# Batching two more chunks of y@w_ch, and sending the seventh chunk's spreads after the last modes

## The chip, the cores and the metric

One core of one Trainium2 chip. A profile is one execution with the hardware profiler on. Its span is shorter than the device time of the same execution, by 1.7 us for the kernel before (453.8 and 455.52), so spans are compared with spans and times with times.

Engines: PE is the matmul engine, ACT the scalar, DVE the vector engine, POOL GpSimd, SP the engine that issues most transfers. SPq, POOLq and DVEq are those engines' sequencers. PSUM is the memory that the matmuls of this program write to; tiles whose names end in _ps lie in it.

## The reference

Causal attention, then a spectral mixing on its output x (8 batches, 576 positions, 512 features, 64 Fourier modes), then a residual with a ReLU:

```python
X = np.fft.rfft(x, axis=1)
# per mode: complex product of X[:, :64] with w_r + i w_i
y = np.fft.irfft(Y, n=S, axis=1)
u = x + y
return u + np.maximum(u @ w_ch, 0.0)
```

The kernel never forms y in time before the product: it computes y@w_ch in the frequency domain and transforms both back.

## The kernel before

The 64 modes are treated in eight chunks, whose weights stream in all the time (the page has the DMA busy 90% or more in the first 36 of its 40 slices). The last feature group yields, for each chunk, a tile `y_sb` of 128 rows (mode, real or imaginary, batch). Two things are needed of it: y itself, and v = y@w_ch, both "spread" so that the modes lie in the partitions of one tile `yv` (16 partitions per chunk, batches along the free axis). Then the inverse transforms are matmuls with `yv` as weights.

There are two ways into `yv`. A chunk can compute its own v and send both by transfers of 128 KB:

```python
if c >= NCK - 2:
    spread(c, 0, yb)           # at the end of modes(): y of the last two chunks
...
def spread(c, which, rows):
    nc.sync.dma_start(out=yv[16 * c : 16 * c + 16, :, which, :], in_=rows)
...
def y_times_wch(c, yt):        # v of one chunk: 4 matmuls, one DVE copy, one transfer
    ...
    nc.vector.tensor_copy(out=vb, in_=vp)
    spread(c, 1, vb)
    return vb
```

Or `gather` takes several chunks' transposed y and makes the rows of `yv` by matmul, batch by batch, each in its own band of partitions, so that no transfer is needed; a round of it is 16 (or 8) matmuls into one PSUM tile and four (or two) copies out of it, on ACT and DVE in turn. Chunks one to four go that way altogether, chunks five and six with y alone:

```python
for c in range(NCK - 2):
    yb = modes(NG - 1, c)
    ...
    yt = y_transposed(yb, c)
    ...
    if c >= NY:
        y_times_wch(c, yt)
        if c == NCK - 3:
            gather(NY, NCK - 2, (), (0,))     # y of chunks five and six, two rounds
    elif c == NY - 1:
        gather(0, NY, (1, 3), (1, 0))         # v and y of chunks one to four
...
c = NCK - 2                                   # the seventh chunk
x_times_wch(0, False)
yb6 = modes(NG - 1, c)
x_transposed(1)
yt = y_transposed(yb6)
x_times_wch(1, False)
vb6 = y_times_wch(c, yt)
...
yb = modes(NG - 1, NCK - 1, {2: first_u, 3: first_z})   # the eighth chunk
```

The first output tiles take chunks seven and eight straight from their tiles (96 rows of `yv` are enough); the first "full" inverse transform reads all 128 rows, and so waits for every spread.

The softmax here doesn't subtract the row's maximum and nothing guards it: scores larger than these inputs give would overflow.

## Time and profile before

| | before |
|---|---|
| time, us (median of 3; range) | 456.47 (455.56 to 456.91) |
| time of the profiled execution | 455.52 |
| span of the profile | 453.8 |
| last matmuls of chunk four's modes start (weights set the pace up to here) | 372.85 |
| modes of chunk five start | 390.79 |
| modes of the eighth chunk start | 411.04 |
| first full inverse transform starts | 421.99 |

The last four rows cut the tail of the kernel into stages. Each is the start of one line of PE's timeline. The chain and the timeline of the batch are shown in the prediction. The transfers from 417 to 425 us: the eighth chunk's two spreads, with the time from issue to landing in the last column.

```profile
yv<-y_sb SPq DMA_DIRECT2D x1, 128.0 KB, 2.9
yv<-v_sb SPq DMA_DIRECT2D x1, 128.0 KB, 2.9
```

### The profile page before, as it was taken

Reading aid. Unit: us, or ns where it says so; the run is one execution under the profiler, and the core shown is the slowest. Engines: PE = TensorE matmul, PEld = TensorE weight load, DVE = VectorE, ACT = ScalarE, POOL = GpSimd, SP = SyncE. Lnnn points to the kernel's source line nnn. Section 1 sums busy time; section 2 is a strip of 40 time slices with the busy share of each in tenths; the row PEclk is TensorE's granted clock in tenths of the full one; section 3 lists DMA queues with packets and bytes.
Section 4 is the critical chain, followed back from the end, with each engine's and each line's share of the span. In section 5 each row is a group of like instructions: output and inputs, shape, how many; then the busy total and the mean of one; then the engine's idle time right before and its main releaser. Section 6 shows DMA issues by size and latency. Waiting matters only on the chain.

```text
span 453.8 us, 10370 instructions
## 1 busy us (share of the span) xinstructions
PE 340.4 (75%) x4233; PEld 218.6 (48%) x4265; DVE 241.0 (53%) x535; ACT 221.9 (49%) x390; POOL 183.0 (40%) x269
## 2 busy tenths in 40 slices
PE   1779887976563979836677857688889678879995
PEld 1456665654342656624445535456554335534332
DVE  7775665753242656723436434446655443562796
ACT  1585877464242656724435444455551323431774
POOL 6655554554344565434364444444433231200000
PEclk9996999998576889968878899889996986999999
DMA  9999999999999999999999999999999999995688
GB/s 176 200 203 203 202 201 204 202 204 204 205 204 202 201 203 202 205 205 204 202 196 203 204 204 203 204 203 202 206 207 208 207 206 206 207 214 109 232 298 317
DMA packets 108511, 93.75 MB, mean 207 GB/s; under 512 B 28384, under 2 KB 103648, under 8 KB 108464
## 3 DMA queue, kind: packets, MB, share of 16 engines
q0 software_dynamic: 98960, 81.81, 113.8%
q1 hardware_dynamic: 9504, 11.29, 7.8%
q8 instruction: 33, 0.54, 0.4%
q14 instruction: 14, 0.11, 0.1%
HBM read 164.56 MB, written 9.44 MB: 383 GB/s over the span
## 4 chain that ended last, share of the span: by engine, by line
DMA 51%; PE 31%; DVE 8%; issue 4%; POOL 2%; ACT 2%; SPq 0%; DVEq 0%; POOLq 0%; ACTq 0%
DMA w_sb<-in_moe_w_i_dram 21%; DMA q<-in_q_dram 15%; DMA w_sb<-in_moe_w_r_dram 11%; PE sc_ps L365 4%; PE av_ps L394 4%; PE z_ps L602 3%; PE yp L441 3%; PE sc_ps L359 3%; PE tr_ps L324 3%; DMA k<-in_k_dram 2%; PE z_ps L693 2%; PE g_ps L652 2%; PE ft_ps L418 2%; PE u_ps L712 2%; PE u_ps L693 1%
## 5 line engine op out<-in xcount | busy, mean ns | idle before, releaser
L373 ACT ACTIVATE p_sb<-sc_ps,cumt_sb 128x576 f16<-128x576 f32 (+1 forms) x256 | 141.7, 635 | 45.6 <-PE sc_ps L365 45.0
L217 POOL DMA_DIRECT2D w_sb<-in_moe_w_i_dram x60 | 45.1, 751 | 85.0 <-PE yp L441 37.6
L217 POOL DMA_DIRECT2D w_sb<-in_moe_w_r_dram x60 | 45.3, 757 | 63.5 <-DMA w_sb<-in_moe_w_r_dram 28.2
L217 POOL DMA_DIRECT2D v<-in_v_dram x72 | 50.8, 708 | 32.0 <-DMA w_sb<-in_moe_w_r_dram 7.4
L324 PE MATMUL tr_ps<-ident,q 64*64 64x64 bf16 x576 | 17.5, 210 | 54.3 <-DMA q<-in_q_dram 54.3
L359 PE MATMUL sc_ps<-negm,ident 128*128 128x256 bf16 x256 | 55.5, 303 | 0.2
L327 DVE COPY qtA<-tr_ps 64x576 bf16<-64x576 bf16 x32 | 23.8, 743 | 49.6 <-PE tr_ps L324 49.5
L441 PE MATMUL yp<-w_sb,xs 128*32 128x512 bf16 x480 | 36.5, 406 | 14.1 <-DMA w_sb<-in_moe_w_i_dram 11.1
L344 ACT ACTIVATE p<-sc_ps,cumt 128x64 f16<-128x64 f32 x32 | 10.0, 313 | 74.3 <-PE sc_ps L340 74.3
L394 PE MATMUL av_ps<-v,p_sb 128*128 128x65 f16 x1024 | 44.5, 198 | 0.0
L394 PEld LDWEIGHTS <-p_sb 128*128 128x128 f16 x1024 | 39.5, 100 | 4.9 <-issue 0.8
L327 DVE COPY ktA<-tr_ps 64x576 bf16<-64x576 bf16 x32 | 24.0, 749 | 33.6 <-PE tr_ps L324 33.6
L324 PEld LDWEIGHTS <-q 64*64 64x64 bf16 x576 | 13.7, 123 | 57.0 <-DMA q<-in_q_dram 56.3
L365 PE MATMUL sc_ps<-qtB,ktB 128*128 128x64 bf16 (+2 forms) x160 | 34.9, 324 | 3.5 <-issue 2.4
L365 PE MATMUL sc_ps<-qtA,ktA 65*128 65x512 bf16 (+2 forms) x192 | 36.5, 299 | 0.7 <-DMA qtA<-ncum_sb 0.7
L399 DVE TENSOR_REDUCE den<-av_ps 128x5 f32<-128x10 f32 x64 | 10.8, 169 | 49.1 <-PE av_ps L394 48.9
L441 PEld LDWEIGHTS <-xs 128*32 128x32 bf16 x512 | 22.6, 170 | 23.8 <-issue 19.8
L404 DVE TENSOR_TENSOR x_all<-av_ps,rcp 128x320 f16<-128x320 f32 x64 | 31.5, 491 | 2.2
L327 ACT COPY ktB<-tr_ps 64x576 bf16<-64x576 bf16 x32 | 20.3, 634 | 20.3 <-DVE ktA L327 19.4
L365 PEld LDWEIGHTS <-ktB 128*128 128x128 bf16 x192 | 22.4, 117 | 14.8 <-issue 6.3
L324 PE MATMUL tr_ps<-ident,k 64*64 64x64 bf16 x576 | 17.3, 209 | 15.3 <-DVE qtB L327 10.7
L602 PE MATMUL z_ps<-wch_sb,xs 128*128 128x512 f16 x96 | 26.1, 421 | 0.2 <-DVE xs L596 0.2
(117 smaller groups left out, 534.8 us busy)
## 6 DMA issues: line engine op xcount, KB each, us to landing
w_sb<-in_moe_w_r_dram POOLq DMA_DIRECT2D x60, 512.0 KB, 11.9
w_sb<-in_moe_w_i_dram POOLq DMA_DIRECT2D x60, 512.0 KB, 11.9
q<-in_q_dram POOLq DMA_DIRECT2D x32, 144.0 KB, 9.9
k<-in_k_dram POOLq DMA_DIRECT2D x32, 144.0 KB, 10.0
v<-in_v_dram POOLq DMA_DIRECT2D x72, 64.0 KB, 9.7
out_dram<-r_sb SPq DMA_DIRECT2D x16, 256.0 KB, 2.2
out_dram<-r_w SPq DMA_DIRECT2D x16, 256.0 KB, 2.6
x_all<-in_moe_w_i_dram POOLq DMA_DIRECT2D x3, 512.0 KB, 9.9
```

Of the source, the lines that this page charges most:

```text
L217: nc.gpsimd.dma_start(out=dst, in_=src)
L324: nc.tensor.transpose(ps[rows, r, :], src[rows, r, :], ident16[rows, rows])
L327: copy(out=dst[n % NQ][rows, :].rearrange("d (p r) -> d p r", r=R), in_=ps[rows].rearrange("d r p -> d p r"),)
L359: nc.tensor.matmul(ps[:, bass.ds(w * S, W)], ident16, negm[:, bass.ts(r, W)], start=True, stop=False, skip_group_check=True,)
L365: nc.tensor.matmul(ps[:, c0 : c0 + i1 - i0], keys[:, w, r, :], qt[:, i0:i1], start=False, stop=True, skip_group_check=True,)
L373: nc.scalar.activation(out=pt[:, poff[x] : poff[x] + S - w * W], in_=ps[:, w * S : (w + 1) * S - w * W], func=ACTF.Exp, bias=cumt_sb[:, x, ...
L394: nc.tensor.matmul(ps[:, I, r : r + NCH], lhsT, rhs, start=(i == 0), stop=(i == len(todo) - 1), skip_group_check=True,)
L399: nc.vector.tensor_reduce(out=den, in_=ps[:, :, 0 : VW : NCH], axis=mybir.AxisListType.X, op=ALU.add)
L404: nc.vector.tensor_tensor(out=x_all[:, g, b, :, D * h : D * h + D], in0=ps[:, :, 1 : NCH], in1=rcp.unsqueeze(2).to_broadcast([P, NT, D]), ...
L441: nc.tensor.matmul(ps[32 * cg : 32 * cg + 32, :], cols[:, c0 : c0 + 32, c * MC + 2 * cg + par], wt[(g, c, ri, par)][:, cg, :], start=(x == ...
L602: nc.tensor.matmul(z[:, x, :], xts[i][:, x, dt, :], wch_sb[:, dt, :], start=(dt == 0), stop=(last and dt == DT - 1), skip_group_check=True,)
L693: nc.tensor.matmul(dst[x][r, :], G_sb[rows, bass.ds(T * P, r.stop - r.start)], yv[rows, bb, which, :], start=start, stop=True, skip_group_ ...
```

## The change

Intent: v of chunks five and six made in the batch too, so that two copies and two transfers among the weights go away; the batch cut into single rounds, put where PE has gaps; and the seventh chunk's two transfers kept out of the stream of weights, since nothing needs them before the first full transform. Core of the diff (cuts marked):

```diff
-            if c >= NCK - 2:
+            if c == NCK - 1:
                 spread(c, 0, yb)
...
         nc.vector.tensor_copy(out=vb, in_=vp)
-        spread(c, 1, vb)
         return vb
-    def gather(c0, c1, turns, kinds):
+    def gather(c0, c1, r, which):            # one round of one kind
...
-                    if g % 2:
-                        nc.vector.tensor_copy(out=dst, in_=src)
...
+            if g == ng - 1:
+                nc.vector.tensor_copy(out=dst, in_=src)
+            else:
+                nc.scalar.copy(out=dst, in_=src)
...
-        if c >= NY:
-            y_times_wch(c, yt)
-            if c == NCK - 3:
-                gather(NY, NCK - 2, (), (0,))
...
+        elif c == NCK - 3:
+            gather(NY, NCK - 2, 0, 1)
+            gather(NY, NCK - 2, 0, 0)
...
     c = NCK - 2
     x_times_wch(0, False)
+    gather(NY, NCK - 2, 1, 1)
     yb6 = modes(NG - 1, c)
     x_transposed(1)
+    gather(NY, NCK - 2, 1, 0)
...
     yb = modes(NG - 1, NCK - 1, {2: first_u, 3: first_z})
+    spread(NCK - 2, 0, yb6)
+    spread(NCK - 2, 1, vb6)
```

More of the change, by code (lines that the diff above doesn't have):

```diff
@@ L645, in gather @@
         ng = P // n
-        for b0 in range(0, B, ng):
-            for which in kinds:
-                ps = auxpool.tile([P, DM], FP32, name="g_ps", tag="aux")
-                for dt in range(DT):
-                    for g in range(ng):
-                        op = yt_first[:, dt, : c1 - c0].rearrange("p c (x b) -> p (c x) b", b=B)
-                        nc.tensor.matmul(
-                            ps[n * g : n * g + n, :] if which else ps[n * g : n * g + n, bass.ts(dt, P)],
-                            op[:, :, b0 + g],
-                            wch_sb[:, dt, :] if which else ident16h,
-                            start=(dt == 0 or not which), stop=(dt == DT - 1 or not which),
-                            tile_position=(0, n * g), skip_group_check=True,
-                        )
-                for g in range(ng):
-                    dst, src = yv[rows, b0 + g, which, :], ps[n * g : n * g + n, :]
-                    if g % 2:
-                        nc.vector.tensor_copy(out=dst, in_=src)
-                    else:
-                        nc.scalar.copy(out=dst, in_=src)
-            if b0 // ng in turns:
-                work()
+        ps = auxpool.tile([P, DM], FP32, name="g_ps", tag="aux")
+        op = yt_first[:, :, : c1 - c0].rearrange("p d c (x b) -> p d (c x) b", b=B)
+        for dt in range(DT):
+            for g in range(ng):
+                nc.tensor.matmul(
+                    ps[n * g : n * g + n, :] if which else ps[n * g : n * g + n, bass.ts(dt, P)],
+                    op[:, dt, :, r * ng + g],
+                    wch_sb[:, dt, :] if which else ident16h,
+                    start=(dt == 0 or not which), stop=(dt == DT - 1 or not which),
+                    tile_position=(0, n * g), skip_group_check=True,
+                )
+        for g in range(ng):
+            dst, src = yv[rows, r * ng + g, which, :], ps[n * g : n * g + n, :]
+            if g == ng - 1:
+                nc.vector.tensor_copy(out=dst, in_=src)
+            else:
+                nc.scalar.copy(out=dst, in_=src)
     ahead = []
@@ L763 @@
             work()
-        if c >= NY:
-            y_times_wch(c, yt)
-            if c == NCK - 3:
-                gather(NY, NCK - 2, (), (0,))
-        elif c == NY - 1:
-            gather(0, NY, (1, 3), (1, 0))
+        if c == NY - 1:
+            for r in range(4):
+                gather(0, NY, r, 1)
+                gather(0, NY, r, 0)
+                if r % 2:
+                    work()
+        elif c == NCK - 3:
+            gather(NY, NCK - 2, 0, 1)
+            gather(NY, NCK - 2, 0, 0)
     assert not order_z and not ahead
```

## The prediction

> **What bounds the kernel now.** I read the chain of waits first, for which resource sets the end in the stretch the change touches; then the timeline of that stretch, engine by engine; then the issues and landings of its transfers.
>
> The page's summary of the chain, then the chain itself from chunk four on (start us, us, what):
>
> ```profile
> DMA 51%; PE 31%; DVE 8%; issue 4%; POOL 2%; ACT 2%; SPq 0%; DVEq 0%; POOLq 0%; ACTq 0%
> ```
>
> ```profile
> 353.00 19.81 DMA w_sb<-in_moe_w_i_dram
> ...
> 396.37 0.92 DVE y_acc L495
> 397.61 0.50 issue
> 398.11 0.69 DVE y_sb L455
> 399.24 1.73 PE z_ps L602 x8
> 400.97 0.86 PE v_ps L633 x4
> 402.29 0.58 ACT yv L664
> 402.89 0.70 DVE yv L662
> 403.61 0.58 ACT yv L664
> 404.22 0.69 DVE yv L662
> 404.94 0.70 DVE yv L662
> 405.66 0.58 ACT yv L664
> 406.27 0.71 DVE yv L662
> 407.00 0.69 DVE y_sb L455
> ```
>
> Weights set the pace up to 372.8 us; nothing of that half is changed. From there TensorE (PE) [...]waits on short hand-offs. Between chunks six and seven the chain is the eight evacuation copies of the batched y (`gather`), strictly one after the other: ScalarE (ACT), VectorE (DVE), ACT, DVE. `y_sb` of chunk seven stands behind the last of them. So the end is set here by PSUM evacuation, not by matmul work or by a transfer.
>
> The timeline of the same place shows what each costs:
>
> ```profile
> 395.13 1.03 PE L633 MATMUL v_ps<-wch_sb,yt_first 128*128 128x512 f16 x4
> 396.08 1.12 PE L441 MATMUL yp<-w_sb,xs 128*32 128x512 bf16 x16
> 397.51 0.68 DVE L637 CAST v_sb<-v_ps 128x512 f16<-128x512 f32 x1
> 401.01 1.01 ACT L492 COPY z<-z_ps 128x1024 f32<-128x1024 f32 x1 [1.09 <-PE z_ps L602]
> 401.76 0.47 PE L652 MATMUL g_ps<-ident16h,yt_first 128*32 128x128 f16 x16
> 403.61 1.17 ACT L664 CAST yv<-g_ps 32x512 f16<-32x512 f32 x2 [0.75 <-DVE yv L662]
> 404.97 1.12 PE L441 MATMUL yp<-w_sb,xs 128*32 128x512 bf16 x16
> 411.04 0.69 PE L441 MATMUL yp<-w_sb,xs 128*32 128x512 bf16 x8
> ```
>
> A 32-partition copy of 512 columns takes 0.58 us on ACT and 0.69 on DVE, no less than one of 128 partitions: cutting a tile into four rows quadruples the evacuation.
>
> The last weight tile. The list of DMA issues, asked for 396 to 397.5 us, gives issue to landing:
>
> ```profile
> w_sb<-in_moe_w_i_dram POOLq DMA_DIRECT2D x1, 512.0 KB, 18.3
> ```
>
> It is issued at 396.87, so it lands near 415.17; its matmuls start at 415.30. PE gets there at the same moment (the 0.42 us before them is put down to "issue", as at other changes of tile width, and not to the DMA). The tile before it, 18.0 us from 393.96, lands near 411.96 and is used at 413.06. So two resources are nearly level: an earlier PE alone would gain about 0.1 us, and an earlier last weight alone gains nothing.
>
> [...]16 matmuls of 32 columns take 1.12 us, the four copies of a round about 2.6. [...]this program guards the whole tile: ACT and DVE never overlap on one tile in the trace. [...]a 128 KB spread takes 6.0 and 6.5 us to land beside the weights, and 2.9 us when they are done.
>
> **The change part by part.** The first batch (chunks one to four) keeps its order on every engine; its two copies per round still go to ACT and DVE. Nothing up to 395.13 moves.
>
> *Chunks five and six lose y@w_ch of their own.* Removed: 2 x 4 matmuls of 512 columns (0.86 us of PE each), 2 DVE copies (0.60 us each back to back) and 2 spreads of 128 KB. Chunk six's modes start 0.86 us earlier, 395.22. But their `y_sb` stands on DVE behind the subtraction that waits for ACT (395.33 + 1.01) and frees DVE only at 397.51. The only thing saved is the `v_sb` copy: `y_sb` starts at 397.51 instead of 398.11, minus 0.60.
>
> *The batch does it instead, in four rounds.* Added: 2 x 16 matmuls of 32 x 512, like those of the modes (1.12 us), so PE is about 0.4 us worse off in all. Copies go from 8 to 16 and are no longer split evenly: three of each four are ACT's (12 x 0.58 = 7.0 us), the fourth is DVE's and waits for ACT's third. The new order on the engines, worked through with the durations above:
>
> PE: transposes of chunk six 398.25, z 398.48, round A (product) 400.30 to 401.42, round B (y) to about 401.85, z of pair 0 to 403.5. ACT: the kept z 400.41 to 401.42, then A 401.48 to 403.23, B 403.23 to 404.98. DVE's fourth: A 403.26 to 403.95, B 405.01 to 405.70.
>
> There are two auxiliary PSUM buffers, so round C (product) may start when A is emptied, 404.00 to 405.12, and the modes of chunk seven when B is, at 405.75 (before: 404.97, so 0.78 late). ACT C 405.18 to 406.93, DVE C 406.96 to 407.65. The built order puts `y_sb` of chunk seven behind DVE C: 407.57 instead of 407.00. Round D (y) on PE 407.70 to 408.17; ACT D 408.23 to 409.98, and only then ACT's transposed copy of chunk seven, done at 410.56. PE meanwhile does pair 1's z from 408.9 to 410.63, so of ACT's delay nothing is left: v of chunk seven starts at 410.63 (before: 410.08), and the last chunk's modes at 411.58 (before: 411.04). Sum: -0.60 gained at `y_sb` of chunk six, +1.14 lost in the copies, net +0.54 us.
>
> *The spreads.* Four of 128 KB leave the stream of weights, two for good and two moved behind the last modes. At the 207 GB/s of that stretch each is 0.63 us, so the last weight should land some 2 to 2.5 us earlier, near 413. It is used at 415.84 by the new times: the relief is real, but hidden. The delayed pair is put between the eighth chunk's y and its v on SyncE's queue, 0.55 us of issue each. The eighth chunk's v was issued at 418.72 and landed 2.9 us later, 421.62, with its reader's weights loaded at 421.77: 0.15 us to spare. Two more transfers stand ahead of it, about 0.5 to 0.7 us of engine time each; as they are issued 0.55 us apart, most is through before it. I allow 0.1 us of new wait.
>
> Sum: +0.54 + 0.1 = about +0.6 us in the profiled execution. What follows 421.7 is unchanged, with PE busy 9.25 of 9.30 us up to 431, so a delay is carried to the end. I take 0.2 off, because in executions other than the profiled one the last weight may be the later of the two and the relief then counts: 456.47 + 0.4 = 456.9 us.
>
> **The rivals.**
>
> *The last weight is what really binds.* It lands within about 0.1 us of its use, and executions of before differ by 1.35 us (455.56 to 456.91). If it is usually late by 1 us, the change turns that wait into slack and PE's +0.54 is what remains: up to 0.5 us faster, 456.0. Against it: no wait for the last weight is charged in this trace.
>
> *Copies overlap better than I worked out.* If ACT keeps ahead and PE's fillers cover the rounds, only -0.60 remains: 455.9. Against it: the two-buffer rule and the order on DVE are built in, and each round must hold a buffer for some 2.4 us.
>
> *ACT becomes the bound.* 12 copies plus the kept z are 8 us in a stretch of about 10; if hand-offs are longer than the 0.03 to 0.06 us seen, each round adds to it and chunk seven's transposed copy delays v: +1.5 us, 458.0.
>
> *The delayed spreads hold up the first full inverse transform.* If the eighth chunk's v queues behind both, it lands 1.0 to 1.3 us late: 457.5 to 458.
>
> **Range and chances.** The parts are all below 1.5 us, against 9.1 us for 2%. The range, 455.4 to 458.3, is the worst rivals on either side plus the spread of single executions. Faster by over 2%: 0.01; within 2%: 0.98; slower by over 2%: 0.01.
>
> **What would show it.** In the timeline: `y_sb` of chunk six near 397.5 and not 398.1 (step one); four rounds of copies of about 2.4 us each, modes of chunk seven near 405.75 and those of chunk eight near 411.6, with the wait before chunk seven put down to a DVE copy of yv; ACT busy nearly throughout from 400.4 to 410.6. In the list of issues: the last weight landing 2 us or more ahead of its use; the eighth chunk's v landing about 3 us after issue. I am wrong if the last chunk's modes start before 410.5 or after 412.5, if the end moves by over 2 us, or if the first half moves at all: the grant of TensorE's clock (0.71 from 372.9 to 390.8) could do that without any of this.

General statements that no trace of this case shows are cut from it. No term of its sum is among them: +0.54 for `y_sb` and the copies, +0.1 for the delayed spreads, about +0.6 in the profiled execution; less 0.2, +0.4 in time. That a copy of 32 partitions takes no less than one of 128 is read off the same profile: ACT's 32x512 copies took 574 ns on average and its 128x512 ones of the transposed y 588; DVE's took 690 and, for v, 687.

## More of the kernel before

The metric is device time in microseconds (us), the median of several executions.

PE's timeline at the first full inverse transform (`128*128`; start us, us). It names no wait: the matmuls before it end just as it starts.

```profile
421.12 1.03 PE L827 MATMUL z_ps<-r_sb,ident16h 128*128 128x512 f16 x4
421.99 0.59 PE L693 MATMUL z_ps<-yv,G_sb 128*128 128x512 f16 x2
```

What SP waits for at the end of the program, after its last store is issued (from 444 us on; us in total, times, longest us):

```profile
SPq L879 <- DMA out_dram<-r_sb: 1.6, 3, 0.6
```

And two rows of the page's table of DMA queues (packets, MB, share of 16 engines):

```profile
q8 instruction: 33, 0.54, 0.4%
q14 instruction: 14, 0.11, 0.1%
```

The page calls their kind `instruction` and counts them with the same 16 DMA engines as the data: 33 packets of 16 KB (q8) and 14 of 8 KB (q14). They are taken here for the engines' own instructions on their way in, and called fetches: q8's for PE's, q14's for other engines', SP's among them. The rows do not say so; runs that change PE's or SP's count test it (e10, x1, x3).

## The result, and the profile after

The changed kernel takes 459.25 us (458.17 to 460.6, six runs), beside 456.54 (455.56 to 457.51, six runs) for the kernel before. The ratio is 1.006, with an interval of 1.0037 to 1.0082. (Ratios here are the mean time of one kernel's fast runs over that of the other's of the same rounds, so not quite the ratio of the medians quoted.) That is within 2%, as predicted, but +2.7 us where +0.4 was predicted, and above the range (455.4 to 458.3). Results are correct.

The page's summary of the chain, to be held against "DMA 51%; PE 31%; DVE 8%" of before:

```profile
DMA 57%; PE 29%; DVE 5%; ACT 3%; issue 3%; POOL 2%; DVEq 0%; POOLq 0%; ACTq 0%
```

DVE's share shrank and DMA's grew. The timeline of the changed kernel, line by line against the prediction: `y_sb` of chunk six, the row of ACT copies, the modes of chunks seven and eight, and the first full inverse transform.

```profile
397.63 0.68 DVE L455 TENSOR_TENSOR y_sb<-yp,y_acc 128x512 f16<-128x512 f32 x1
401.56 5.42 ACT L661 CAST yv<-g_ps 32x512 f16<-32x512 f32 x9
405.86 1.12 PE L441 MATMUL yp<-w_sb,xs 128*32 128x512 bf16 x16 [0.68 <-DVE yv L659]
411.78 0.69 PE L441 MATMUL yp<-w_sb,xs 128*32 128x512 bf16 x8
424.17 0.60 PE L688 MATMUL z_ps<-yv,G_sb 128*128 128x512 f16 x2 [1.28 <-DMA yv<-v_sb]
```

The first four are within 0.2 us of the predicted 397.51, 401.48, 405.75 and 411.58. The fifth carries a wait of 1.28 us that was not there before, and the chain of waits goes through it:

```profile
419.45 4.67 DMA yv<-v_sb
424.12 0.05 issue
424.17 0.60 PE z_ps L688 x2
```

The eighth chunk's v needs 4.67 us to land instead of 2.9. So far that is rival four. But the end is later as well. The stages:

| stage, us | before | after | difference |
|---|---|---|---|
| chunk five's modes to the eighth's | 20.25 | 20.88 | +0.63 |
| eighth's modes to first full transform | 10.95 | 12.39 | +1.44 |
| first full transform to the end | 31.81 | 32.43 | +0.62 |
| sum | | | +2.69 |

The sum is the difference of the medians (2.7; the two spans differ by 2.8). The half before (372.85 and 372.71 for chunk four's last matmuls) did not move. In the last stage PE does the same work in the same time (busy 26.06 us before, 26.07 after); what differs is SP's wait for the last stores, the same view as before:

```profile
SPq L882 <- DMA out_dram<-r_sb: 2.3, 3, 1.1
```

The longest wait is 1.1 us, was 0.6. The stores land late (those from r_sb of 256 KB 2.7 us after issue in the median, 2.2 before). Asked for half a microsecond at a time, the list of transfers has one instruction packet in each of the two places: the first line is of 421 to 421.5 us, in the middle of the spreads; the second of 451 to 451.5, on the first of the last four stores (issued at 450.89).

```profile
q8 instruction: 1, 0.02, 22.4%
...
q14 instruction: 1, 0.01, 4.4%
```

By their records in the trace the first packet took 1.79 us (22.4% of 16 x 0.5) and the second 0.35 (4.4%). In the kernel before the same fetches fall at 423.5 to 424 (1.73 us), when its last spread had landed (421.6), and at 446.5 to 447 (0.40 us), ahead of the last four stores (448.70). The other 32 packets of q8 took 0.89 to 1.05 us in both traces. The change has 46 more PE instructions and four fewer SP instructions (8594 to 8640, 236 to 232 in the built programs). The theory is that this shifts where in the work each next fetch falls. Not shown is how a fetch would hold up a transfer, and the trace does not name the engine of a packet, so this link is the author's guess; that the landing is late when such a packet falls on it is what the runs test.

### The profile page after: what moved, and what is told of

Its sections match the earlier page's. It is cut to its first block, busy times and chain, and to the rows that moved or that the text cites. A ratio compares the mean times of both kernels' runs of the same rounds, so it can differ in the third digit from the quotient of the medians.

```text
span 456.6 us, 10452 instructions
## 1 busy us (share of the span) xinstructions
PE 344.5 (75%) x4289; PEld 218.5 (48%) x4289; DVE 239.2 (52%) x533; ACT 227.0 (50%) x398; POOL 183.2 (40%) x269
## 4 chain that ended last, share of the span: by engine, by line
DMA 57%; PE 29%; DVE 5%; ACT 3%; issue 3%; POOL 2%; DVEq 0%; POOLq 0%; ACTq 0%
DMA w_sb<-in_moe_w_i_dram 29%; DMA q<-in_q_dram 13%; DMA w_sb<-in_moe_w_r_dram 5%; PE yp L441 5%; PE sc_ps L365 4%; PE av_ps L394 3%; PE sc_ps L359 3%; DMA x_all<-in_moe_w_r_dram 2%; DMA k<-in_k_dram 2%; PE tr_ps L324 2%; PE z_ps L688 2%; DMA y_acc<-in_moe_w_i_dram 2%; PE ft_ps L418 2%; DMA y_acc<-in_moe_w_r_dram 2%; PE z_ps L514 2%
## 5 line engine op out<-in xcount | busy, mean ns | idle before, releaser
L365 PE MATMUL sc_ps<-qtB,ktB 128*128 128x512 bf16 (+2 forms) x192 | 44.8, 351 | 0.0
L324 PE MATMUL tr_ps<-ident,k 64*64 64x64 bf16 x576 | 17.5, 210 | 14.1 <-DVE qtB L327 10.1
```

The costliest lines, as they stand in the source:

```text
L324: nc.tensor.transpose(ps[rows, r, :], src[rows, r, :], ident16[rows, rows])
L365: nc.tensor.matmul(ps[:, c0 : c0 + i1 - i0], keys[:, w, r, :], qt[:, i0:i1], start=False, stop=True, skip_group_check=True,)
```

## The experiments

Theories. **Copies** (C in the texts): the four-quadrant copies cost 0.63. **Row** (Q): four spreads in a row slow one another. **Fetch** (F): the displaced instruction fetches cost some 0.6 each, on the eighth chunk's v and on the last stores. Two more letters stand in the texts: W and R, that the relief of the last weights is worth something. The rival to all is what the total alone would suggest: the new batch costs 2.7 us, being longer than worked out. The stages of all runs are in one table at the end of this section.

### e1_early_spreads and e2_late_spreads: the two halves of the change apart

e1 is the changed kernel with the seventh chunk's spreads at their old places:

```diff
-            if c == NCK - 1:
+            if c >= NCK - 2:
                 spread(c, 0, yb)
...
+        spread(c, 1, vb)
         return vb
...
-    spread(NCK - 2, 0, yb6)
-    spread(NCK - 2, 1, vb6)
```

e2 is the kernel before with only these two spreads late:

```diff
-            if c >= NCK - 2:
+            if c == NCK - 1:
                 spread(c, 0, yb)
...
-        spread(c, 1, vb)
+        if c < NCK - 2:
+            spread(c, 1, vb)
...
+    spread(NCK - 2, 0, yb6)
+    spread(NCK - 2, 1, vb6)
```

> The changed kernel with the seventh chunk's two spreads put back where they were (each issued as soon as its rows are ready); the batch in four rounds stays. Theory Q (queue): most of the 2.7 us come from the four spreads standing in one row, which let the eighth chunk's v land 4.67 us after issue instead of 2.9; with the row gone it lands in about 2.9 us, the wait of 1.28 us before the first full inverse transform is gone, the last chunk's modes stay near 411.8, and the time is 0.5 to 1.0 us over before (456.5), so near 457.2. Theory C (copies): the sixteen copies and ScalarE's load cost the time, now or through what follows; then it stays 2 us or more over before. Theory W (weights): the delay of the spreads was worth something by letting the last weight land earlier; then the last weight lands after 415 again and a wait for it appears.

> The kernel before with only the seventh chunk's two spreads delayed behind the last modes; y@w_ch of chunks five and six as before. Theory Q: the eighth chunk's v lands 4 to 5 us after issue, PE waits 1.2 to 2 us for it, and the time is 1.5 to 2.2 us over before. Theory C: no more than 0.5 us over before, since no copy is added. Theory W: faster than before by some 0.1 us or more.

e1: 457.99 us, ratio 1.0027 (1.001 to 1.0043). e2: 456.93, ratio 1.0008 (0.9991 to 1.0024). The late spreads alone are not 2 us, and without them half the loss stays. In e2's profile the full transform waits 0.69 us; its stage is 0.85 us longer than before, and the end is not (31.80). In e1, with a single spread of v as before, it still waits. The lines of e2 and of e1:

```profile
423.20 0.61 PE L694 MATMUL z_ps<-yv,G_sb 128*128 128x512 f16 x2 [0.69 <-DMA yv<-v_sb]
```

```profile
422.79 0.60 PE L689 MATMUL z_ps<-yv,G_sb 128*128 128x512 f16 x2 [0.54 <-DMA yv<-v_sb]
```

e1's v took 3.9 us to land instead of 2.9, with no other spread near. What was near: v was issued at 418.81, and from 419.5 to 420 us the only packet on the engines is an instruction fetch, which starts just ahead of the spread's own packets and takes 1.5 us (18.8% of 16 x 0.5).

```profile
DMA packets 1, 0.02 MB, mean 33 GB/s; under 512 B 0, under 2 KB 0, under 8 KB 0
...
q8 instruction: 1, 0.02, 18.8%
```

So the row of four costs 0.85 (e2), and something else that goes with the new batch costs 0.7 at the same place and 0.6 at the end (e1: 32.41, longest wait for a store 1.1).

### e4_doubled and e5_wide: what is slow in a row of four

Both are the kernel before with its early spreads kept, plus two transfers of 128 KB after the last modes: e4 sends the narrow ones (16 partitions) a second time, e5 sends the same tiles whole, into 128 partitions of a spare tile.

```diff
+    spread(NCK - 2, 0, yb6)                                    # e4
+    spread(NCK - 2, 1, vb6)
```

```diff
+    for i, src in enumerate((yb6, vb6)):                       # e5
+        nc.sync.dma_start(out=y_acc[:, 4 + i, : DM // 2].bitcast(FP16), in_=src)
```

> The kernel before with the same two spreads issued a second time behind the last modes (same rows, same values; the early ones stay). The relief of the weights is away, the row of four at the end is there. Theory Q: as late as the run with only the delay, 1.5 to 2.2 us over before. If the relief of the weights matters, it is slower than that run by what the relief is worth. Theory C: at most 0.3 us over before.

> The kernel before with two extra transfers of 128 KB at the same place, from the same tiles, but into 128 partitions of a spare tile instead of 16. It tells two forms of theory Q apart. Q1: what holds the eighth chunk's v is the number of bytes and packets ahead of it in the queue; then it lands as late as with the doubled spreads (4 us or more after issue) and costs the same 1.5 us or so. Q2: what holds it is that many rows go into few partitions, which a single spread hides and a row of four doesn't (packets went from about 60 to 160 ns in the changed kernel's trace); then wide transfers let it land in 2.9 to 3.5 us and cost under 0.7 us.

e4: 456.87, 1.0006 (0.9992 to 1.0021); e5: 456.29, 0.9998 (0.9974 to 1.0021). The times are too close; the profiles are not. e4's full transform waits 0.66 us, e5's not at all (10.96, as before). (e4's stage is 12.65: it also holds waits of 0.41 and 0.35 us for the last two weights, which come back below.) The lists of transfers of e2 and of e5, 417 to 425.4 us in 40 slices of 0.21 us, show the rate:

```profile
GB/s 0 0 0 0 0 49 205 283 112 190 283 122 210 185 112 112 107 98 127 102 102 68 205 195 176 322 361 419 410 400 380 419 400 410 419 302 234 49 0 0
```

```profile
GB/s 0 0 0 0 0 0 0 0 0 0 0 24 161 288 147 258 297 59 302 293 44 0 137 254 220 15 0 0 68 419 380 429 371 419 380 234 380 410 420 439
```

In e2 the first half of the row goes mostly at 185 to 283 GB/s, and then eight slices in a row at about 105. The trace of the changed kernel, which has the same row, shows it packet by packet: from the middle of the third narrow spread on, the 1 KB packets take 145 to 167 ns (means of 64 records), against 49 to 64 in the first. In e5, with the wide ones in between, each of the four peaks at 250 to 300 and is through, with pauses between them. So what slows is several narrow spreads without a pause, not the bytes and not the issues. Why the narrow ones slow is not shown.

### e6_pe_shift, e8_both_shift, e9_before_shifted: instruction counts moved, clumsily

e6 is the changed kernel with 23 small transposes of the attention part, far ahead, done twice (46 PE instructions). e8 adds six SP instructions. e9 is the kernel before with the same 23 transposes, and four SP loads moved to ACT's queue.

```diff
                 nc.tensor.transpose(ps[rows, r, :], src[rows, r, :], ident16[rows, rows])
+                if n == 6 and 2 * r + h < (12, 11)[which]:                  # e6, e8, e9
+                    nc.tensor.transpose(ps[rows, r, :], src[rows, r, :], ident16[rows, rows])
...
-    nc.sync.dma_start(out=ident16h, in_=d_ident16h)
+    for _ in range(5):                                                      # e8
+        nc.sync.dma_start(out=ident16h, in_=d_ident16h)
...
+    nc.scalar.dma_start(out=ident16h, in_=d_ident16h)                       # e9 (and Ff_sb, G_sb, ident32)
```

> The changed kernel with 46 harmless instructions more on TensorE, early, where it waits for transfers (23 transposes of the seventh head pair done twice). Theory F (fetch): the change, by its 46 more TensorE instructions, moved one 16 KB transfer of TensorE's own instructions (queue 8 of the profile) onto the spread of the eighth chunk's v[...]; 46 more move it ahead of the spreads. Then the eighth chunk's v lands about 4.1 us after issue (as with the delayed spreads alone) instead of 4.7, PE's wait shrinks from 1.28 to about 0.7 us, and the time is 0.4 to 0.8 us below the changed kernel's 459.25, near 458.6. Theory Q alone: no change, within 0.3 us. Extra work costs: slower than the changed kernel.

> As the run before it, and SyncE given six instructions more, early (a small constant loaded four times again), so that the last 8 KB transfer of instructions (queue 14), which in the changed kernel and in the one with early spreads fell among the last stores, comes before them again. Theory F: from the first full inverse transform to the end of the span 31.8 us again (as before) instead of 32.4; the time another 0.4 to 0.7 us lower, near 458.0, that is 1.3 to 1.7 us over before: 0.6 of copies and 0.8 of the row of four spreads are left. Theory Q alone: no change against the changed kernel.

> The kernel before, with nothing of the change, but with the instruction counts of the changed kernel: 46 more on TensorE (early, repeated transposes) and 4 fewer on SyncE (four constants loaded from ScalarE's queue). Theory F: the eighth chunk's v lands 3.7 us or more after issue, a wait of about 0.5 us for it appears, the end after the first full inverse transform takes 32.4 us instead of 31.8, and the time is 0.8 to 1.3 us over before, near 457.5. Without theory F: within 0.3 us of before.

e6: 459.34, 1.0064 (1.0044 to 1.0084). e8: 460.15, 1.0079 (1.0056 to 1.0102). e9: 456.45, 1.0000 (0.9983 to 1.0017). All three totals missed what the fetch theory expected. In e6 the shift put the fetch just ahead of the row instead of on it, and the wait stayed 1.11. In e8 chunk four's last matmuls start at 376.91, not 372.7, presumably because of the five loads at the very start, so its total cannot be read; and a fetch of PE fell among the stores at 448.69 us, 12 us before the end. In e9 the profile shows all that the fetch theory expected (v landing 3.9 us after issue, a wait of 0.53 for it, 32.32 us to the end), and a wait of 1.02 us for a weight besides:

```profile
412.97 0.45 PE L443 MATMUL yp<-w_sb,xs 128*32 128x512 bf16 x4 [1.02 <-DMA w_sb<-in_moe_w_i_dram]
```

Yet e9's time is that of the kernel before; why is not known. A shift has to be aimed: the same count as before but for a whole block, the instructions of one packet, and by a means that costs nothing at the front. The block was taken as 256 PE instructions. That is the author's estimate: 33 packets of q8 for 8594 instructions (before) and for 8640 (after) are one for every 260 and 262.

### e10_before_pe46 and e11_after_aligned: the shift aimed

e10 is the kernel before with just the 46 more PE instructions, one per call. e11 is the changed kernel with 210 more (46 + 210 = 256, one block by that estimate, so the fetches should fall where they did in the kernel before) and four more SP instructions, by cutting two small transfers of two heads in two. (The cut transfers bring two PE instructions more, so the built program has 258 over the kernel before.)

```diff
                 nc.tensor.transpose(ps[rows, r, :], src[rows, r, :], ident16[rows, rows])
+                if 0 < n and 2 * r + h < 1 and 1 * (2 * n - 2 + which) + 2 * r + h < 23:    # e10
+                if 0 < n and 2 * r + h < 2 and 2 * (2 * n - 2 + which) + 2 * r + h < 105:   # e11
+                    nc.tensor.transpose(ps[rows, r, :], src[rows, r, :], ident16[rows, rows])
...
-        nc.sync.dma_start(out=qtA[n % NQ][D : D + 1, :], in_=ncum_sb[p0 : p0 + 1, :])
+        for cols in (slice(0, S // 2), slice(S // 2, S)) if n in (5, 6) else (slice(0, S),):   # e11
+            nc.sync.dma_start(out=qtA[n % NQ][D : D + 1, cols], in_=ncum_sb[p0 : p0 + 1, cols])
```

> The kernel before with only 46 TensorE instructions more (23 transposes done twice, one at a time, spread over the first half), so that the 16 KB transfer of TensorE's instructions falls where it falls in the changed kernel. Theory F: the eighth chunk's v lands 3.7 to 4.0 us after issue, and from the start of chunk eight's modes to the first full inverse transform it takes 11.5 to 11.8 us instead of 10.95; from there to the end 31.8 as before, because SyncE's count is untouched; the time 0.5 to 0.9 us over before. Without F: 10.95 and the time within 0.3 us of before.

> The changed kernel with the instruction counts brought back to where before has them modulo the size of a fetch: 210 more on TensorE (105 transposes done twice, two at a time over the first half), 4 more on SyncE (four tiny row loads cut in two). The last shifts failed because one transfer fell just ahead of the row of spreads, and another among the stores. Theory F: 11.8 us from chunk eight's modes to the first full inverse transform (12.39 in the changed kernel; the row of four alone gave 11.80) and 31.8 from there to the end (32.43); the time 1.0 to 1.5 us below the changed kernel, 457.7 to 458.2. Without F: as the changed kernel, 459.3.

e10: 457.12, ratio 1.0012 (0.9995 to 1.0029). Nothing near the end of this kernel differs from the kernel before, and yet its full transform waits; the list of transfers has v landing after 3.9 us, and a fetch between 422 and 422.5.

```profile
424.62 0.60 PE L695 MATMUL z_ps<-yv,G_sb 128*128 128x512 f16 x2 [0.49 <-DMA yv<-v_sb]
```

The stage is 12.31, a miss (11.5 to 11.8 was expected): PE also waits for the last two weights, as it does not in the profile of the kernel before. After these, from the transposes of the eighth chunk's y to the full transform, it takes 6.33 us for 5.68 before, so 0.65 of the 1.36 by which the stage grew is the fetch's. The end is as before (31.78).

```profile
414.77 0.46 PE L443 MATMUL yp<-w_sb,xs 128*32 128x512 bf16 x4 [0.36 <-DMA w_sb<-in_moe_w_i_dram]
417.31 0.45 PE L443 MATMUL yp<-w_sb,xs 128*32 128x512 bf16 x4 [0.24 <-DMA w_sb<-in_moe_w_i_dram]
```

e11: 457.42, ratio 1.0022 (1.0 to 1.0045): the ratio goes from 1.0060 to 1.0022, some 1.7 of the 2.7 us, by adding 216 instructions that do nothing useful (the two intervals just overlap). Its fetches fall at 425.5 to 426 and at 449 to 449.5, clear of both places. The wait at the full transform is what e2 had, and the last stores wait 0.6 again:

```profile
424.37 0.61 PE L691 MATMUL z_ps<-yv,G_sb 128*128 128x512 f16 x2 [0.75 <-DMA yv<-v_sb]
```

```profile
SPq L885 <- DMA out_dram<-r_sb: 1.5, 3, 0.6
```

The rival, that the batch costs 2.7 us, falls: the batch is all there.

### x1_after_sp4 and x3_after_sp6: SP's fetch alone

x1 is the changed kernel with e11's four SP instructions only. x3 loads the constant five times, as e8 did, and leaves PE's count alone.

> The changed kernel with nothing altered but four more SyncE instructions far ahead of the part in question (the transfers of two cumulative rows of two heads are each cut in two), so that SyncE's instruction count is that of the kernel before. Theory F (the fetch of SyncE's own instructions[...] falls among the last four stores because the change took four instructions from SyncE): the longest wait at the end for a store goes back from 1.1 to 0.6 us and the stretch from the first full inverse transform to the end from 32.4 to 31.8; the wait for the eighth chunk's v (1.28) and the last chunk's modes (20.9 us after chunk five's) stay. Timed: 458.6, 0.6 under the changed kernel's 459.25. Rival (the end is longer because more stores queue up after the late full transform, whatever the fetch does): the end stays 1.1 and 32.4, and the time 459.2.

> The changed kernel with six more SyncE instructions (one small constant is loaded five times instead of once, at the very start) and TensorE's count unchanged, because x1 had two more TensorE instructions and with them a 34th fetch of TensorE's stream. Theory F: SyncE's last but one fetch falls ahead of the last four stores, the longest wait for a store at the end is 0.6 us and the stretch from the first full inverse transform to the end 31.8, not 32.4; the wait for v stays near 1.3. Timed 458.6, ratio about 1.0047. Rival (the end is longer for another reason): wait 1.1, stretch 32.4, time 459.2, ratio 1.006.

x1: 458.79, 1.0051 (1.0033 to 1.0069), near the value expected, but its profile shows another thing. Cutting the transfers brought two more PE instructions, 8642, and with them a 34th packet in q8, where the changed kernel has 33. It came at 450 to 451 us, while one store's issue took 1.71 us instead of 0.33 (SP's timeline, then that window's transfers):

```profile
450.34 1.71 SPq L744 DMA_DIRECT2D out_dram<-r_w  x1
```

```profile
q8 instruction: 1, 0.02, 9.6%
```

The longest wait for a store is 0.6, as expected, but the stage is 33.50. That the fetch held the issue is not shown by a run of its own, but the traces agree on it: after 405 us, by reading of SP's timelines, no issue of SP's in any of the twenty takes over 0.64 us unless a fetch of PE's is on its way; with one it took 0.66 us in the kernel before (424.99), 1.46 in the changed kernel (421.84), 1.35 in e6, 1.59 and 1.79 in e8, and elsewhere as little as 0.33. So a fetch of PE's may also delay what SP sends.

x3: 459.45, 1.0076 (1.0055 to 1.0098), a miss in the total: like e8 it loads the constant five times, and it comes late to chunk four (374.91; e5, without such loads, has 374.65, so the loads are not shown to be the cause). Its last stage is the clean test, with the wait for v kept (1.10): 31.71 us and

```profile
SPq L883 <- DMA out_dram<-r_sb: 1.5, 3, 0.6
```

So in the profile SP's fetch alone is worth 0.7 us of the last stage (32.43 to 31.71).

### x2_copies_alone: what is left of the change without row and fetches

e1 with e11's alignment (both diffs above).

> The changed kernel with the seventh chunk's two spreads back in their early places and with the added instructions of e11 (210 for TensorE, four for SyncE, both far ahead), so that neither fetch is where it does harm and there is no row of four spreads: of the change only the new batch and its copies are left. If the decomposition is complete, the last chunk's modes start 20.87 us after chunk five's, the full inverse transform 10.95 us after that with no wait for v, the end 31.7 us after that: +0.62 us in all, timed 457.0, a ratio of about 1.0014. If something else of the change costs time (its 16 more TensorE instructions near the end, ScalarE's larger load), more than 1.0025 and the stage that shows it is longer than in the kernel before.

The stages are 20.87 and 10.95 with no wait, to a hundredth as expected, and then 31.62 (31.7):

```profile
423.08 0.59 PE L692 MATMUL z_ps<-yv,G_sb 128*128 128x512 f16 x2
```

Only the copies' 0.62 is left. Yet the time is 455.95, ratio 0.9993 (0.9979 to 1.0007): no loss at all, where 1.0014 was expected.

### y1_relief_alone, y2_relief_early_zeros, y3_spreads_twice: does the relief of the weights pay for the copies?

y1 and y2 are the kernel before without the four spreads that the change takes out of the stream of weights (a wrong result; their rows are zero, which the tolerance let pass). y3 sends them twice.

```diff
-            if c >= NCK - 2:
+            if c == NCK - 1:                    # y1, y2
                 spread(c, 0, yb)
...
-        spread(c, 1, vb)                        # y1, y2: gone; y3: for _ in range(2)
...
+    nc.vector.memset(yv[64:96, :, 1, :], 0.0)   # y1, ahead of the loop over chunks
+    nc.vector.memset(yv[96:112, :, :, :], 0.0)
+        if c < 3:                               # y2, inside it
+            for b in range(3 * c, min(3 * c + 3, B)):
+                nc.vector.memset(yv[64:P, b, :, :], 0.0)
```

> Wrong result on purpose: the kernel before, with the spreads that the change takes out of the stream of weights (the products of chunks five and six, both spreads of chunk seven) left out altogether and their rows set to zero by two early memsets, SyncE's count kept. All copies and all matmuls stay as before, so of the change only the relief of the last weights is left. Theory R (in most executions the last weights are late by some tenths of a us to 1 us, though not in the profiled one of before; the relief then counts and hides the copies' 0.62): 455.8 to 456.0, a ratio of 0.9985 to 0.999, and in the profile no wait for a weight after the last chunk's modes have begun. Rival (the weights are in time and x2's 455.95 is chance): 456.3 to 456.5, ratio 1.000.

> As y1 (the kernel before, wrong result on purpose: the spreads of the products of chunks five and six and both of chunk seven left out, their rows zero), but the rows are zeroed in eight short pieces during chunks one to three instead of two long ones that held VectorE up by 5 us, and SyncE's count of 236 is kept by cutting eight small transfers of the attention part in two. Theory R (in most executions the last weights are late, and the relief counts): 455.6 to 456.0, ratio 0.998 to 0.999, in the profile no wait for weights after the last chunk's modes have begun. Rival (weights are in time): 456.1 to 456.4, ratio 0.9995 to 1.0005.

> The kernel before with the same four spreads sent twice in their early places (same data to the same rows): the other sign. Four more transfers of 128 KB at the 207 GB/s of that stretch are 2.5 us of the engines. Theory R: the last weights are later by up to that, PE waits for them after the last chunk's modes have begun, and the time is 457.5 to 458.5, ratio 1.003 to 1.005. Rival (the weights have slack in most executions, or the spreads fill gaps): 456.2 to 456.8, ratio 1.000 to 1.001.

y1: 464.49, 1.019 (1.0176 to 1.0203), and no answer: its two memsets took 3.47 and 1.77 us of DVE, and chunk four came at 381.99. y2: 456.46, 0.9995 (0.9973 to 1.0018), which is the rival's number, but its interval holds both. y3: 460.94, 1.0092 (1.0072 to 1.0111), more than either theory, and not for the reason named: no wait for weights, but 1.96 us at an inverse transform for doubled spreads of v, and another 1.04 at the full one. So no timed run shows the relief to be worth anything. The profiles show more. After the eighth chunk's modes have begun, PE waits for the last two weights for 0.76 us in e4, 1.02 in e9 and 0.60 in e10. These keep the four spreads in the stream of weights, as do the kernel before, e5 and y3, which have no such wait: 0.4 us on average of the six. (b1 has 0.32, but its PE comes 1 us sooner.) In all thirteen profiles of kernels with two or four of these spreads taken out or delayed there is none. So the profile of the kernel before, of a quick execution (455.52 us for a median of 456.5), may be a lucky one, and an average execution of it would pay something that x2 does not. By this estimate 0.4 of the copies' 0.62 would be hidden in time; that it is so, and the rest, stays open. A part may be chance: chunk four's last matmuls start between 372.5 and 374.7 us in the profiles without loads added at the start.

### c2_later_round, c2_aligned, b1_split_rounds: towards a better version

With the copies the only real cost, one can move a round. c2 is e1 with the second product round behind the seventh chunk's own v, where PE has slack; c2_later_round has e8's counts, c2_aligned e11's. b1 is the kernel before with its second y round moved behind the seventh chunk's modes.

```diff
-    gather(NY, NCK - 2, 1, 1)                         # c2
     yb6 = modes(NG - 1, c)
...
     vb6 = y_times_wch(c, yt)
+    gather(NY, NCK - 2, 1, 1)
```

```diff
-                gather(NY, NCK - 2, (), (0,))         # b1
+                gather(NY, NCK - 2, (), (0,), (0,))
...
     x_transposed(1)
+    gather(NY, NCK - 2, (), (0,), (1,))
```

> A version meant to beat both: early spreads for the seventh chunk, and the second product round of the batch moved from ahead of chunk seven's modes to behind its v, so that chunk seven's modes wait for one round of copies less; instruction counts shifted as in the second run. If the copies that hold the two auxiliary buffers are what made chunk eight's modes 0.63 us later, these now start 20.0 us or less after chunk six's (before 20.25, changed 20.88), and the time is 0.2 to 0.5 us below before, near 456.2. If ScalarE's load in itself is what costs, they stay near 20.9 us and the time near 457.1.

> The version with early spreads and one product round moved behind chunk seven's v, with the instruction counts of the run before it. Its copies gave 19.90 us from chunk five's modes to chunk eight's (before 20.25). Theory F with the copies theory: then 10.95 and 31.8, so 0.35 us below before in these stages, time 455.8 to 456.4. If the fetches are not what cost, the end stays at 32.4 and the time at 456.7 to 457.4.

> The kernel before with one thing of the change: the second round of copies of chunks five's and six's y is moved from ahead of chunk seven's modes to behind them; everything else, spreads and products included, is as before, and TensorE's and SyncE's counts are the same within two. If the eight copies in one chain hold PE, chunk eight's modes start up to 1 us earlier (19.2 to 19.6 us after chunk five's instead of 20.25); the last weight then becomes the bound (it landed 0.1 us ahead of its use), so at most 0.5 us of it is left at the end: 455.9 to 456.5. If the copies are hidden anyway: 20.25 and no change.

c2_later_round: 457.42, 1.0032 (1.0009 to 1.0055), a miss: its middle stages were as hoped, but a fetch of PE fell among its stores 12 us before the end (443.16; the last stage is 32.38), and it had the five loads. c2_aligned: 455.84, 0.999 (0.9975 to 1.0005), the lowest time of all, though not clear of the kernel before. b1: 456.71, 1.0009 (0.9994 to 1.0024), a miss: the eighth chunk's modes are 1.04 us nearer to chunk five's (19.21), but 0.32 of that goes to a wait for the last weights at once, and the rest does not show in the time.

### The stages of the runs

Each column is read off PE's timeline as in the table of the kernel before; the last column is the longest wait for a store.

| run | five to eight | eight to full (wait for v) | full to end | store |
|---|---|---|---|---|
| before | 20.25 | 10.95 (none) | 31.81 | 0.6 |
| after | 20.88 | 12.39 (1.28) | 32.43 | 1.1 |
| e2: row alone | 20.25 | 11.80 (0.69) | 31.80 | 0.6 |
| e1: no row | 20.87 | 11.66 (0.54) | 32.41 | 1.1 |
| e11: no fetches in the way | 20.87 | 11.86 (0.75) | 31.63 | 0.6 |
| x3: only SP's fetch moved | 20.85 | 12.23 (1.10) | 31.71 | 0.6 |
| x2: copies alone | 20.87 | 10.95 (none) | 31.62 | 0.6 |
| c2_aligned | 19.88 | 10.88 (none) | 31.59 | 0.6 |

Differences of rows give the terms: copies 0.62 (x2 less before, first column); row 0.91 (e11 less x2, second column) or 0.85 (e2 less before); PE's fetch 0.53 (after less e11, second column); SP's fetch 0.7 (after less x3, last stage). Sum 2.7 to 2.8.

These are terms of single profiles. In time, the ratios of the changed kernel, e11 and x2 (1.0060, 1.0022, 0.9993) give 1.7 us for the two fetches together, 1.3 for the row and -0.3 for the copies, each uncertain by about 1 us. One fetch by itself is seen in profiles alone: e9 and e10, with a fetch moved onto v, are not clear of the kernel before in time (1.0000 and 1.0012).

## Why the prediction was wrong

*`y_sb` of chunk six 0.60 earlier, the copies +1.14, net +0.54.* Right: 397.63 for 397.51; the eighth chunk's modes +0.63 measured from chunk five's. The order of the built program on ACT and DVE, worked through with single durations, was good to 0.2 us over sixteen copies. (The sum for PE had a slip: 2 x 1.12 less 2 x 0.86 is 0.5 us, not 0.4. Nothing rested on it.) ACT was busy nearly throughout, nine copies in 5.42 us, without becoming a bound of its own.

*The relief of the last weight is real but hidden.* Right in the profile, if smaller: issued at 396.12 us, the weight landed 17.5 us later, at 413.65, for a use at 416.04. That is 1.6 us earlier than before, not 2 to 2.5; the rest of the 2.4 us to spare is PE coming later. The first rival, that the last weight binds in other executions, was real in part: e4, e9 and e10 wait 0.6 to 1.0 us for weights. The 0.2 us taken off for it is neither shown nor refuted in time (x2 for it, y2 for neither).

*The first half does not move.* Right.

*"I allow 0.1 us of new wait" for the delayed spreads.* This is the step that failed. The mechanism stood among the rivals, as the fourth, with 1.0 to 1.3 us late; the eighth chunk's v landed 2.5 us later than before (424.12 for 421.62), and the stage grew by 1.44. The term was mis-sized for two reasons. It took "0.5 to 0.7 us of engine time each" for all four spreads and so found most of it gone before v's issue; the runs showed that from the middle of the third on a row of narrow ones goes at about 105 GB/s, half the rate of the first two (e2, e4, against e5): 0.85 to 0.91. And it did not ask what else the DMA engines carry: PE's instruction fetch fell on v's own spread, 0.53 more (e1, e10, e11).

*"What follows 421.7 is unchanged."* Failed too: PE's work is unchanged, the stores are not. The four SP instructions that the change removes moved a fetch of 8 KB into the last four stores, 0.6 to 0.7 us (x3). The prediction's own sign of being wrong, an end moved by over 2 us, came true: 456.6 for 453.8.

Of the +2.7, then, by the stages of the profiles, the predicted mechanism made 0.6, a rival that was judged nearly harmless 0.9, and some 1.2 an effect that has nothing to do with what the change computes.

## What to carry to other kernels

When a change moves the tail by a microsecond or two, look at the instruction packets in the list of DMA queues before explaining it by the work. Here 46 more PE instructions, all in the first half, moved a packet of q8 from 1.6 us behind the start of the first full transform to over 2 us ahead of it (e10), and an aimed padding (256 of PE's, four of SP's, e11) told some 1.7 us of such a loss from the rest. Spreads into 16 partitions, queued in a row right ahead of the one that the path waits for, cost 0.85 to 0.91 us here (e2, e11). And a gain or a cost in the stages of one profile is not yet one in time: here the stages of x2 (+0.43 in all) and of b1 (-0.67) said 0.7 and 1.1 us otherwise than their ratios (-0.3 and +0.4). Before a profile serves as the base of every difference, see whether its execution was a typical one.
